# Transposing the 64x64 corner of each attention row tile on VectorE instead of TensorE

## The chip, the cores and the metric

The kernel runs on one core of a Trainium2 chip. The metric is the time of one execution in microseconds (us), measured on the device; smaller is better. Besides the timed runs there is one profiled execution, from which all rows below are taken. The engines are called as in the profile: PE (TensorE, matmuls), PEld (its weight loads), DVE (VectorE), ACT (ScalarE), POOL (GpSimd) and SP (it issues the DMAs).

## The reference, cut to what matters

Three layers follow each other, in float32. The first is a causal attention with 32 heads (batch 4, 8 heads, 576 tokens, 64 columns each):

```
scores = scale * np.matmul(q, k.transpose(0, 1, 3, 2))
scores = np.where(causal, -1000000000.0, scores + np.minimum(bias, 0.0))
attn = np.exp(scores - np.max(scores, axis=-1, keepdims=True))
attn = attn / (np.sum(attn, axis=-1, keepdims=True) + 1e-09)
return np.matmul(attn, v)
```

The second mixes tokens by a rank-32 product and applies a feed-forward layer (512 to 2048 to 512). The third is a causal attention again, with 16 heads (4 batches, 4 experts), whose probabilities are multiplied by a gate; then comes an output product. The change touches only the step between the two products of an attention, where the probabilities have to be transposed so that the sum over keys runs over partitions.

## The kernel before

The program has three stages. The first attention fills the time to about 300 us; beside it, as fillers, run the conversion of weights that arrive as 64-bit words, the token mixing and part of the feed-forward layer. The feed-forward layer alone takes 300 to 680 us. The second attention, with its projections, takes the rest. Both attentions use the class `Attn`.

A head's 576 rows are cut in five row tiles t = 0 to 4. Tile 0 has 64 rows, the others 128; tile t sees 64, 192, 320, 448 or 576 keys (`WID`), because of causality. So tile t has t full blocks of 128x128, and at its right end one 64x64 corner on the diagonal, of which the lower triangle counts. Tile 0 is only a corner.

`run` goes through steps, five for a head. Step i does, in this order: the score product of tile i on PE (`qk`), the transposition of a tile of the head two before it (`tr`, since `LAG` is 10 steps), then on DVE the masked scores with their row maximum (`peak`, L363), on ACT the exponential of the step before (`exp`, L370), and the copies of the transposed tile from PSUM into the buffer `pt` (`evac`, through `cp`: L77 on ACT, L79 on DVE). Once for a head, at its successor's second step, `norm` computes the reciprocals (L375 and L376 on DVE) and has POOL scale all five row tiles (L381). After two heads `push_pv` queues the product with V (L420). The fillers of a step stand behind all that. Each engine works its instructions in program order, so an instruction that waits holds back all behind it.

`TRP` says what the transposing step r = 0 to 4 of a head does: step 0 transposes the full block of tile 1 and the corners of tiles 0 and 1, step 1 tile 2 with its corner, step 2 tile 3 with its corner, step 3 tile 4, step 4 the corner of tile 4. Full blocks are transposed at L393, corners at L396; both go through PE as products with an identity matrix into a PSUM tile `t`, of which there are two in turn. The copy of a corner is a second instruction of `evac`. `ENGA` and `ENGG` name the engine of each copy in the first and the second attention, for even and odd heads; a is ACT, v is DVE. The probabilities lie in two buffers P, for even and odd heads; `pt` has three.

Of the kernel before, what the change touches and what calls it, by code (L numbers as in the profile page):

```python
# [8 lines left out]
F32 = mybir.dt.float32  # L9
# [9 lines left out]
B, H, S, D = 4, 8, 576, 64  # L19
DM, DFF, E, R = 512, 2048, 4, 32  # L20
P = 128
NP = H // 2
NT = 5
# [5 lines left out]
ROWS = [64, 128, 128, 128, 128]  # L29
I0 = [0, 64, 192, 320, 448]  # L30
WID = [64, 192, 320, 448, 576]
OFF = [0, 64, 256, 576, 1024]
PW = 1600
KB = [128, 128, 128, 128, 64]
HALF = S // 2
THIRD = S // 3
# [2 lines left out]
PST = 448  # L39
# [12 lines left out]
STREAM = (((0, 0), (2, -3)), ((-1, 4),), ((0, 1),), ((0, 2), (1, -2)), ((1, -1),), ((0, 3),))  # L52
FAST = (40, 70)

ENGA = ('vaaaaa', 'aavaav')
ULA = "gvgg"
WLE = "g"

HALVES = 152
UFIRST = 161  # L60
WIDE = (7,)
ENGG = ('aaaava', 'aaaava')

GTAB = "kkkkvvvvvqqqq......."
GATE = (9, 5, 2)
OB = "avava"
XG = 0

TRP = ((1, 0, 2), (2, 2, 3), (3, 3, 4), (4, 0, 0), (0, 4, 5))
BG = (1, 1, 0, 2, 1)  # L70
SPLIT = 7
ULF = "vggg"
# [77 lines left out]
def fused_kernel(ctx, tc, qk, v, s, u, vv, w12, wp, out):  # L150
    nc = tc.nc
    cst = ctx.enter_context(tc.tile_pool(name="cst", bufs=1))

    ident = cst.tile([P, P], F32, name="ident")
# [162 lines left out]
    class Attn:  # L317
# [5 lines left out]
        def __init__(self, pools, nq, engines, scale, split=0):  # L323
            self.nq, self.scale, self.split = nq, scale, split
            self.engines = engines
            self.st, self.psq, self.pst = pools
            self.pt = [self.st.tile([P, PTW], F32, name=f"pt{i}") for i in range(3)]
            self.stat, self.P = [], []
# [4 lines left out]
            for i in range(2):  # L333
                self.P.append(self.st.tile([P, PW], F32, name=f"P{i}"))
                nc.gpsimd.memset(self.P[i][0:64, 0:64], 0.0)
            self.pvq = []

        def clear(self, i):


            nc.gpsimd.memset(free_ap(self.pt[i][64:128], 0, [[PST + P, NT], [1, 64]]), 0.0)

        def qk(self, n, t):
            q1, k1, q2, k2 = self.pair_ready(n)
# [11 lines left out]
        def peak(self, n, t, view):  # L356

            M, W = ROWS[t], WID[t]
            stat = self.stat[n % 3]
            po, mk = self.P[n % 2][P - M:, OFF[t]:OFF[t] + W], mask[P - M:, S - W:]  # L360
            if len(view.shape) > 2:
                po, mk = (x.rearrange("p (a b) -> p a b", a=2) for x in (po, mk))
            nc.vector.tensor_tensor_reduce(out=po, in0=view, in1=mk, scale=-self.scale, scalar=3.0e38, op0=OP.add,  # L363
                                           op1=OP.min, accum_out=stat[P - M:, 0, t:t + 1])

        def exp(self, n, t):
            M, W = ROWS[t], WID[t]
            stat = self.stat[n % 3]
            po = self.P[n % 2][P - M:, OFF[t]:OFF[t] + W]
            nc.scalar.activation(out=po, in_=po, func=AF.Exp, scale=-1.0, bias=stat[P - M:, 0, t:t + 1],  # L370
                                 accum_out=stat[P - M:, 1, t:t + 1])

        def norm(self, n):
            stat = self.stat[n % 3]
            nc.vector.tensor_scalar(out=stat[:, 2, :], in0=stat[:, 1, :], scalar1=1e-9, scalar2=None, op0=OP.add)  # L375
            nc.vector.reciprocal(out=stat[:, 2, :], in_=stat[:, 2, :])  # L376
            gate = self.heads[n].get("gate")
            for t in range(NT):
                r0 = P - ROWS[t]
                pv = self.P[n % 2][r0:, OFF[t]:OFF[t] + WID[t]]  # L380
# [3 lines left out]
        def tr(self, n, r):  # L384

            ps = self.pst.tile([P, 512], F32, tag="t", name=f"t_{n}_{r}")
            Pn = self.P[n % 2]
            t, a, e = TRP[r]  # L390
            for kb in range(t):
                c0 = OFF[t] + P * kb
                nc.tensor.transpose(ps[:, P * kb:P * kb + P], Pn[:, c0:c0 + P], ident)  # L393
            for k in range(a, e):
                c0, x = OFF[k] + WID[k] - 64, P * (t + k - a)
                nc.tensor.transpose(ps[0:64, x:x + P], Pn[:, c0:c0 + 64], ident)  # L396
            return ps

        def evac(self, n, r, ps):
            pt = self.pt[n % 3]  # L400
            t, a, e = TRP[r]
            if t:
                cp(nc, self.engines[n % 2][r], free_ap(pt[:, :], I0[t], [[PST, t], [1, P]]), ps[:, :P * t])
# [36 lines left out]
        def run(self, pair_ready, pv_done, heads, fillers):  # L440
            self.pair_ready, self.pv_done, self.heads = pair_ready, pv_done, heads
            n = len(self.heads) * NT
            i = 0
            while i < n + self.LAG or self.pvq:
                j = i - self.LAG
                view = self.qk(i // NT, i % NT) if i < n else None
                ps = self.tr(j // NT, j % NT) if 0 <= j < n else None
                if i < n:
                    self.peak(i // NT, i % NT, view)
                if 1 <= i <= n:  # L450
                    self.exp((i - 1) // NT, (i - 1) % NT)
# [12 lines left out]
                i += 1  # L464
# [465 lines left out]
    with ExitStack() as cx:  # L930
# [148 lines left out]
        def g_out(b, kb):  # L1079
# [10 lines left out]
            if b < B - 1:  # L1090
                ob = d2.tile([P, DM], F32, tag="ob", name=f"ob_{b}_{kb}")
            else:
                ob = attn.P[kb % 2][:, DM * (kb // 2):DM * (kb // 2) + DM]
# [126 lines left out]
```

## Time and profile before

| | us |
|---|---|
| median of 3 timed runs (851.15 to 851.56) | 851.36 |
| the profiled execution's own time | 849.59 |
| its span, first to last instruction | 847.8 |
| PE busy | 804.4 |
| PEld busy | 743.4 |
| DVE busy | 522.2 |
| ACT busy | 478.3 |
| POOL busy | 329.7 |

Busy time is time in which the engine executes at least one instruction. A matmul and the load of its weights overlap, and so do neighbouring matmuls, so PE's busy time is not its load in columns. An idle engine costs time only where the others wait for it.

### The profile page before, as it was taken

The numbers are of one execution on the slowest core, as the hardware profiler recorded it, in microseconds if no ns is written. First come the engines' busy times: TensorE is split into PE (matmuls) and PEld (weight loads), VectorE is DVE, ScalarE is ACT, GpSimd is POOL, SyncE is SP. The second block draws the span as 40 slices with busy tenths as digits, with TensorE's granted clock in tenths as the row PEclk, the third lists the DMA queues.
The fourth block names the chain that finished last, engine by engine and source line by source line (L and its number), as shares of the span: only waits on it lengthen the run. The fifth ranks groups of instructions, "written<-read, shape, count | busy, mean of one in ns | idle before, by whom it ended". The sixth has DMA issues, their size and how long they took to land.

```text
span 847.8 us, 17359 instructions
## 1 busy us (share of the span) xinstructions
PE 804.4 (95%) x6068; PEld 743.4 (88%) x6068; DVE 522.2 (62%) x1547; ACT 478.3 (56%) x1446; POOL 329.7 (39%) x498
## 2 busy tenths in 40 slices
PE   4898799999999999999999999999999989999997
PEld 3676588988888799999999999999999989898875
DVE  7778876786665457646554664464456775656541
ACT  6788777776676445334434443443333576666672
POOL 6656655453453335223422442232333043322241
PEclk9999999999999999999999999999999999999999
DMA  7877566646651151112121221110000221212121
GB/s 212 220 214 208 167 171 187 198 134 169 184 134 44 37 210 51 50 27 55 45 63 26 77 59 42 50 39 26 1 1 2 43 44 29 67 42 54 53 65 62
DMA packets 35897, 75.48 MB, mean 89 GB/s; under 512 B 4584, under 2 KB 8168, under 8 KB 35780
## 3 DMA queue, kind: packets, MB, share of 16 engines
q1 hardware_dynamic: 35812, 74.39, 32.2%
q8 instruction: 48, 0.79, 0.4%
q14 instruction: 37, 0.30, 0.1%
HBM read 38.93 MB, written 8.55 MB: 56 GB/s over the span
## 4 chain that ended last, share of the span: by engine, by line
PE 77%; DVE 5%; ACT 3%; POOL 2%; issue 2%; DMA 0%; SPq 0%; POOLq 0%; DVEq 0%; ACTq 0%
PE hps L836 21%; PE facc L854 21%; PE pv L420 6%; PE qkp L1064 5%; PE t L393 4%; PE facc L298 3%; PE ops L1087 3%; PE hps L284 3%; PE vps L997 3%; PE qk L353 2%; PE qk L352 2%; PE t L396 2%; POOL P L381 2%; DVE P L363 1%; ACT pt L77 1%
## 5 line engine op out<-in xcount | busy, mean ns | idle before, releaser
L268 POOL TENSOR_TENSOR ul<-uT,uh 128x288 fp32r<-128x288 f32 x126 | 101.7, 826 | 172.0 <-ACT uh L267 149.0
L370 ACT ACTIVATE P<-P,stat 64x64 f32<-64x64 f32 (+4 forms) x240 | 133.7, 557 | 44.1 <-DVE stat L363 42.0
L841 DVE SCALAR_TENSOR_TENSOR hl<-hps,hh 128x288 fp32r<-128x288 f32 x110 | 50.4, 458 | 150.0 <-ACT hh L840 150.0
L381 POOL TENSOR_SCALAR P<-P,stat 64x64 f32<-64x64 f32 (+4 forms) x160 | 101.4, 648 | 104.6 <-DVE stat L376 58.1
L363 DVE CUSTOM_DVE_ANT_0 P<-qk,mask 64x64 f32<-64x64 f32 (+4 forms) x240 | 116.4, 487 | 37.6 <-PE qk L353 21.9
L840 ACT ACTIVATE hh<-hps 128x288 fp32r<-128x288 f32 x110 | 45.0, 409 | 147.9 <-PE hps L836 147.6
L77 ACT ACTIVATE pt<-t 64x64 f32<-64x64 f32 (+5 forms) x304 | 89.8, 336 | 41.3 <-PE t L396 35.3
L836 PE MATMUL hps<-uh,wl 128*128 128x288 f32 x376 | 111.2, 296 | 0.0
L836 PE MATMUL hps<-ul,wh 128*128 128x288 f32 x376 | 111.1, 296 | 0.0
L854 PE MATMUL facc<-hh,wh 128*128 128x288 f32 x376 | 111.1, 296 | 0.0
L836 PE MATMUL hps<-uh,wh 128*128 128x288 f32 x376 | 111.0, 295 | 0.0
L854 PE MATMUL facc<-hh,wl 128*128 128x288 f32 x376 | 110.9, 295 | 0.0
L854 PE MATMUL facc<-hl,wh 128*128 128x288 f32 x376 | 110.8, 295 | 0.0
L352 PE MATMUL qk<-R,L 128*128 128x288 f32 (+4 forms) x288 | 94.9, 334 | 16.4 <-DVE L L577 9.6
L393 PE MATMUL t<-ident,P 128*128 128x128 f32 x480 | 88.1, 282 | 11.4 <-ACT pt L77 4.8
L381 POOL TENSOR_SCALAR P<-P,stat,pt 64x64 f32<-64x64 f32 (+4 forms) x80 | 48.5, 620 | 113.1 <-DVE stat L376 57.6
L393 PEld LDWEIGHTS t<-ident,P 128*128 128x128 f32 x480 | 58.8, 142 | 23.3 <-issue 9.4
L352 PEld LDWEIGHTS qk<-R,L 128*128 128x128 f32 x288 | 57.0, 198 | 23.9 <-issue 11.8
L420 PE MATMUL pv<-pt,V 128*64 128x288 f32 (+4 forms) x752 | 76.9, 344 | 0.0
L191 POOL TENSOR_TENSOR wl<-c_a_w,wh 128x256 fp32r<-128x256 f32 x56 | 43.7, 781 | 76.8 <-ACT wh L188 74.2
L836 PEld LDWEIGHTS hps<-uh,wl 128*128 128x128 f32 x376 | 70.9, 189 | 0.0
L854 PEld LDWEIGHTS facc<-hh,wl 128*128 128x128 f32 x376 | 70.9, 188 | 0.0
(186 smaller groups left out, 2145.6 us busy)
## 6 DMA issues: line engine op xcount, KB each, us to landing
c_raw_w<-in_w_dram SPq DMA_DIRECT2D x64, 256.0 KB
uT<-in_qk_dram SPq DMA_DIRECT2D x15, 576.0 KB
L<-HI SPq DMA_DIRECT2D x28, 288.0 KB
V<-in_v_dram SPq DMA_DIRECT2D x16, 320.0 KB
R<-HI SPq DMA_DIRECT2D x14, 288.0 KB
R<-uT SPq DMA_DIRECT2D x14, 288.0 KB
L<-uT SPq DMA_DIRECT2D x14, 288.0 KB
aD<-stage SPq DMA_DIRECT2D x6, 576.0 KB
```

The lines of the kernel that those rows point to most:

```text
L77: nc.scalar.activation(out=out, in_=in_, func=AF.Copy)
L268: eng.tensor_tensor(out=l_, in0=src, in1=h_.bitcast(F32), op=OP.subtract)
L352: nc.tensor.matmul(ps[:, bk, :w], lhsT=q1[:, rows], rhs=k1[:, c0:c0 + w], start=True, stop=False)
L363: nc.vector.tensor_tensor_reduce(out=po, in0=view, in1=mk, scale=-self.scale, scalar=3.0e38, op0=OP.add, op1=OP.min, accum_out=stat[P - M: ...
L370: nc.scalar.activation(out=po, in_=po, func=AF.Exp, scale=-1.0, bias=stat[P - M:, 0, t:t + 1], accum_out=stat[P - M:, 1, t:t + 1])
L381: nc.gpsimd.tensor_scalar(out=pv, in0=pv, scalar1=stat[r0:, 2, t:t + 1], scalar2=1.0 if gate is None else gate(t)[r0:], op0=OP.mult, op1=O ...
L393: nc.tensor.transpose(ps[:, P * kb:P * kb + P], Pn[:, c0:c0 + P], ident)
L420: nc.tensor.matmul(out[64 * hh:64 * hh + 64, lo - a:e - a], lhsT=V(hh, kb), rhs=pt[:, PST * kb + lo:PST * kb + e], start=kb == 0, stop=kb ...
L836: nc.tensor.matmul(ps, lhsT=w[:, 0, cs], rhs=x, start=i == 0, stop=i == 11)
L840: nc.scalar.activation(out=hh, in_=ps, func=AF.Relu)
L841: nc.vector.scalar_tensor_tensor(out=hl, in0=ps, scalar=0.0, in1=hh.bitcast(F32), op0=OP.max, op1=OP.subtract)
L854: nc.tensor.matmul(accs[c][d], lhsT=w[:, 1, cs], rhs=x, start=f == fs[0] and i == 0, stop=f == fs[-1] and i == 2)
```

## The change

The corners are no longer transposed by PE. `corners` has DVE transpose them in blocks of 32x32 directly from P to `pt`, both in SBUF: the two blocks on the diagonal of a corner and the one under it; the fourth is all zeros, and `clear` zeroes its place once. One instruction takes the same block of three tiles (0 to 2, at step 0) or two tiles (3 and 4, at step 2), so there are three instructions at either step. For that the two buffers P become one, in which the corners of a head lie at equal distances. PE transposes tiles 1, 2, 4 and 3 at steps 0 to 3 and nothing at step 4. All copies out of the PSUM tiles `t` are made by ACT.

```
-ENGA = ('vaaaaa', 'aavaav')
+ENGA = ('aaaa', 'aaaa')
-ENGG = ('aaaava', 'aaaava')
+ENGG = ('aaaa', 'aaaa')
-TRP = ((1, 0, 2), (2, 2, 3), (3, 3, 4), (4, 0, 0), (0, 4, 5))
+TRP = (1, 2, 4, 3)
+CORNERS = {0: (0, 3), 2: (3, 5)}
...
             nc.gpsimd.memset(free_ap(self.pt[i][64:128], 0, [[PST + P, NT], [1, 64]]), 0.0)
+            nc.gpsimd.memset(free_ap(self.pt[i][32:64], 0, [[PST + P, NT], [1, 32]]), 0.0)
...
-            for k in range(a, e):
-                c0, x = OFF[k] + WID[k] - 64, P * (t + k - a)
-                nc.tensor.transpose(ps[0:64, x:x + P], Pn[:, c0:c0 + 64], ident)
...
-            if e > a:
-                cp(nc, self.engines[n % 2][r], free_ap(pt[0:64], (PST + P) * a, [[PST + P, e - a], [1, 64]]),
-                   free_ap(ps[0:64], P * t + 64, [[P, e - a], [1, 64]]))
+        def corners(self, n, a, e):
+
+            c0, step = DIAG[n % 2]
+            pt = self.pt[n % 3]
+            for q, k in ((0, 0), (32, 0), (32, 32)):
+                nc.vector.transpose(out=free_ap(pt[k:k + 32], (PST + P) * a + q, [[PST + P, e - a], [1, 32]]),
+                                    in_=free_ap(self.P[64 + q:96 + q], c0 + step * a + k, [[step, e - a], [1, 32]]))
...
-                ps = self.tr(j // NT, j % NT) if 0 <= j < n else None
+                ps = self.tr(j // NT, TRP[j % NT]) if 0 <= j < n and j % NT < len(TRP) else None
+                if 0 <= j < n and j % NT in CORNERS:
+                    self.corners(j // NT, *CORNERS[j % NT])
```

On PE, in the middle of the first attention, steps 0, 2, 3 and 4 of one head; `qk` are score tiles, `t` the PSUM tiles of the transpositions. Before:

```order
L393 MATMUL t_0_2063<-ident,P_114 128x128
L396 MATMUL t_0_2063<-ident,P_114 64x128 x2
...
L393 MATMUL t_2_2132<-ident,P_114 128x128 x3
L396 MATMUL t_2_2132<-ident,P_114 64x128
L352 MATMUL qk_3_2145<-R_1_127,L_1_125 128x448
L353 MATMUL qk_3_2145<-HI,L_1_128 128x448
L393 MATMUL t_3_2148<-ident,P_114 128x128 x4
...
L396 MATMUL t_4_2183<-ident,P_114 64x128
```

And on PE at the same places of the change:

```order
L394 MATMUL t_1_1999<-ident,P 128x128
...
L394 MATMUL t_4_2066<-ident,P 128x128 x4
L357 MATMUL qk_3_2081<-R_1_124,L_1_122 128x448
L358 MATMUL qk_3_2081<-HI,L_1_125 128x448
L394 MATMUL t_3_2084<-ident,P 128x128 x3
```

The five corner transpositions of the head are gone, and tile 4 is transposed before tile 3 (`t` is numbered by the step before, and by the row tile now).

On DVE, from the same head's step 0 to its step 2, before (`ISA` is `peak`, in two instructions; the rows of other lines are fillers and the reciprocals):

```order
L363 ISA P_114,stat_108<-qk_0_2060,mask 64x64
L363 ISA stat_108 64x1
L79 COPY pt_106<-t_0_2063 128x128
L79 COPY pt_106<-t_0_2063 64x2x64
L113 SCALAR_TENSOR_TENSOR pt_107<-pt_105,pt_106 128x256
L253 TENSOR_TENSOR uT<-mo_1_1_2078,uT 128x288
...
L494 TENSOR_TENSOR uT<-uT,HI 128x576
L649 TENSOR_TENSOR stage_2058<-facc_1_2118,uT 128x288
L363 ISA P_114,stat_108<-qk_2_2129,mask 128x320
L363 ISA stat_108 128x1
```

And the same stretch of DVE in the change:

```order
L406 STREAM_TRANSPOSE pt_106<-P 32x3x32 x3
L368 ISA P,stat_108<-qk_0_1996,mask 64x64
L368 ISA stat_108 64x1
L115 SCALAR_TENSOR_TENSOR pt_107<-pt_105,pt_106 128x256
L255 TENSOR_TENSOR uT<-mo_1_1_2014,uT 128x288
...
L497 TENSOR_TENSOR uT<-uT,HI 128x576
L652 TENSOR_TENSOR stage_1994<-facc_1_2052,uT 128x288
L406 STREAM_TRANSPOSE pt_106<-P 32x2x32 x3
L368 ISA P,stat_108<-qk_2_2063,mask 128x320
L368 ISA stat_108 128x1
```

The copies behind `peak` are gone, and the transposes of the corners stand right ahead of the `peak` of tiles 0 and 2.

## Rows read from the trace of the kernel before

**Rows 1.** The page's first part: busy us, share of the span, instructions.
```profile
PE 804.4 (95%) x6068; PEld 743.4 (88%) x6068; DVE 522.2 (62%) x1547; ACT 478.3 (56%) x1446; POOL 329.7 (39%) x498
```

**Rows 2.** Busy time by stretch: length; PE, PEld, DVE, ACT, POOL; clock, DMA share, GB/s.
```profile
20.00:120.00 100.00, 84.80 (x606) 65.66 (x607) 78.37 (x260) 79.70 (x271) 61.56 (x90) 0.98 0.72 195
120.00:280.00 160.00, 157.00 (x1261) 141.29 (x1261) 112.50 (x365) 114.00 (x368) 77.00 (x120) 1.00 0.56 149
280.00:300.00 20.00, 17.84 (x149) 14.05 (x148) 6.95 (x20) 9.73 (x29) 6.92 (x11) 1.00 0.31 104
680.00:848.00 168.00, 158.46 (x1184) 138.51 (x1182) 89.67 (x321) 104.27 (x321) 50.69 (x89) 1.00 0.19 51
```

**Rows 3.** The same of tile t alone: transpositions (PE, PEld), copies (DVE, ACT).
```profile
20.00:120.00 100.00, 33.23 (x186) 20.61 (x186) 7.43 (x26) 21.66 (x74) 0.98 0.72 195
120.00:280.00 160.00, 44.69 (x267) 29.52 (x267) 9.92 (x34) 31.69 (x108) 1.00 0.56 149
280.00:300.00 20.00, 4.36 (x27) 2.87 (x27) 1.15 (x4) 3.48 (x12) 1.00 0.31 104
680.00:848.00 168.00, 39.55 (x240) 25.90 (x240) 3.40 (x16) 32.94 (x112) 1.00 0.19 51
```

**Rows 4.** The chain of waits that ended last, by line, from 120 to 280 us.
```profile
by line: PE facc L298 16.6%; PE hps L284 14.9%; PE pv L420 11.1%; PE t L393 9.2%; PE qk L353 7.2%; PE qk L352 6.8%; PE t L396 5.4%; POOL P L381 5.3%; PE mx L227 3.6%; issue 3.1%; PE mt L239 2.9%; PE mo L250 1.7%; ACT pt L77 1.6%; POOL ul L2
```

**Rows 5.** The same chain from 680 to 848 us.
```profile
by line: PE qkp L1064 19.5%; PE pv L420 15.3%; PE ops L1087 15.2%; PE t L393 9.6%; PE vps L997 8.5%; PE qk L353 5.1%; PE qk L352 4.8%; PE t L396 4.4%; issue 2.6%; ACT pt L77 2.0%; DVE P L363 2.0%; ACT P L370 1.7%; POOL P L381 1.7%; DVE L L1
```

**Rows 6.** Pieces of the chain in order of time: start, us, engine and line.
```profile
152.20 0.11 PE qk L353
152.31 0.17 PE t L393
152.48 0.22 PE t L396 x2
152.69 0.27 PE mo L250 x2
```

**Rows 7.** Groups by shape, DVE: busy us, mean ns of one, idle before, releaser.
```profile
L79 DVE COPY pt<-t 128x384 f32<-128x384 f32 x16 | 8.8, 552 | 0.8 <-PE t L396 0.7
L79 DVE COPY pt<-t 64x64 f32<-64x64 f32 x32 | 6.7, 209 | 3.6 <-PE t L396 3.5
L79 DVE COPY pt<-t 128x128 f32<-128x128 f32 x16 | 4.7, 292 | 0.5
L79 DVE COPY pt<-t 64x128 f32<-64x128 f32 x16 | 4.4, 273 | 0.0
L375 DVE TENSOR_SCALAR stat<-stat 128x5 f32<-128x5 f32 x48 | 9.2, 191 | 6.6 <-ACT P L370 6.4
L668 DVE TENSOR_TENSOR U<-c_a_u,U 128x160 fp32r<-128x160 f32 x2 | 0.8, 438 | 0.0
```

**Rows 8.** Groups by shape, ACT's copies out of t.
```profile
L77 ACT ACTIVATE pt<-t 64x64 f32<-64x64 f32 x112 | 23.1, 206 | 1.2 <-PE t L396 1.1
L77 ACT ACTIVATE pt<-t 128x384 f32<-128x384 f32 x32 | 15.6, 486 | 28.4 <-PE t L396 28.4
L77 ACT ACTIVATE pt<-t 128x128 f32<-128x128 f32 x32 | 8.5, 266 | 1.9 <-PE t L396 1.5
L77 ACT ACTIVATE pt<-t 64x128 f32<-64x128 f32 x32 | 8.3, 260 | 0.0
```

**Rows 9.** POOL in order of time: start, us of the five scalings of a head.
```profile
22.54 4.01 POOL L381 TENSOR_SCALAR P<-P,stat 64x64 f32<-64x64 f32 x5 [0.46 <-DVE stat L376]
...
190.76 3.32 POOL L381 TENSOR_SCALAR P<-P,stat 64x64 f32<-64x64 f32 x5 [1.26 <-DVE stat L376]
```

**Rows 10.** DVE in order of time: start, us.
```profile
21.16 0.48 DVE L79 COPY pt<-t 128x128 f32<-128x128 f32 x2
...
28.06 0.49 DVE L363 CUSTOM_DVE_ANT_0 P<-qk,mask 128x320 f32<-128x320 f32 x1
...
201.03 0.23 DVE L363 CUSTOM_DVE_ANT_0 P<-qk,mask 64x64 f32<-64x64 f32 x1
```

More of the change, by code (lines that the diff above doesn't have):

```diff
@@ L31 @@
 WID = [64, 192, 320, 448, 576]
-OFF = [0, 64, 256, 576, 1024]
-PW = 1600
+SLOT = 640
+OFF = [[SLOT * t for t in range(5)], [SLOT * (5 - t) - WID[t] for t in range(5)]]
+DIAG = [(WID[0] - 64, SLOT + P), (SLOT * 5 - 64, -SLOT)]
 KB = [128, 128, 128, 128, 64]
@@ L327, in __init__ @@
             self.pt = [self.st.tile([P, PTW], F32, name=f"pt{i}") for i in range(3)]
-            self.stat, self.P = [], []
+            self.stat = []
             for i in range(3):
@@ L332, in __init__, with rows @@
                 self.stat.append(t)
-            for i in range(2):
-                self.P.append(self.st.tile([P, PW], F32, name=f"P{i}"))
-                nc.gpsimd.memset(self.P[i][0:64, 0:64], 0.0)
+            self.P = self.st.tile([P, SLOT * NT], F32, name="P")
             self.pvq = []
+        def rows(self, n, t):
+            c0 = OFF[n % 2][t]
+            return self.P[P - ROWS[t]:, c0:c0 + WID[t]]
         def clear(self, i):
             nc.gpsimd.memset(free_ap(self.pt[i][64:128], 0, [[PST + P, NT], [1, 64]]), 0.0)
+            nc.gpsimd.memset(free_ap(self.pt[i][32:64], 0, [[PST + P, NT], [1, 32]]), 0.0)
         def qk(self, n, t):
@@ L359, in peak @@
             stat = self.stat[n % 3]
-            po, mk = self.P[n % 2][P - M:, OFF[t]:OFF[t] + W], mask[P - M:, S - W:]
+            po, mk = self.rows(n, t), mask[P - M:, S - W:]
             if len(view.shape) > 2:
@@ L366, in exp @@
         def exp(self, n, t):
-            M, W = ROWS[t], WID[t]
+            M = ROWS[t]
             stat = self.stat[n % 3]
-            po = self.P[n % 2][P - M:, OFF[t]:OFF[t] + W]
+            po = self.rows(n, t)
             nc.scalar.activation(out=po, in_=po, func=AF.Exp, scale=-1.0, bias=stat[P - M:, 0, t:t + 1],
@@ L379, in norm, with tr @@
                 r0 = P - ROWS[t]
-                pv = self.P[n % 2][r0:, OFF[t]:OFF[t] + WID[t]]
+                pv = self.rows(n, t)
                 nc.gpsimd.tensor_scalar(out=pv, in0=pv, scalar1=stat[r0:, 2, t:t + 1],
                                         scalar2=1.0 if gate is None else gate(t)[r0:], op0=OP.mult, op1=OP.mult)
[L384 to L390, printed above, removed]
+        def tr(self, n, t):
+            ps = self.pst.tile([P, 512], F32, tag="t", name=f"t_{n}_{t}")
+            Pt = self.rows(n, t)
             for kb in range(t):
-                c0 = OFF[t] + P * kb
-                nc.tensor.transpose(ps[:, P * kb:P * kb + P], Pn[:, c0:c0 + P], ident)
-            for k in range(a, e):
-                c0, x = OFF[k] + WID[k] - 64, P * (t + k - a)
-                nc.tensor.transpose(ps[0:64, x:x + P], Pn[:, c0:c0 + 64], ident)
+                nc.tensor.transpose(ps[:, P * kb:P * kb + P], Pt[:, P * kb:P * kb + P], ident)
             return ps
         def evac(self, n, r, ps):
+            t = TRP[r]
+            cp(nc, self.engines[n % 2][r], free_ap(self.pt[n % 3][:, :], I0[t], [[PST, t], [1, P]]), ps[:, :P * t])
+        def corners(self, n, a, e):
+            c0, step = DIAG[n % 2]
             pt = self.pt[n % 3]
-            t, a, e = TRP[r]
-            if t:
-                cp(nc, self.engines[n % 2][r], free_ap(pt[:, :], I0[t], [[PST, t], [1, P]]), ps[:, :P * t])
-            if e > a:
-                cp(nc, self.engines[n % 2][r], free_ap(pt[0:64], (PST + P) * a, [[PST + P, e - a], [1, 64]]),
-                   free_ap(ps[0:64], P * t + 64, [[P, e - a], [1, 64]]))
+            for q, k in ((0, 0), (32, 0), (32, 32)):
+                nc.vector.transpose(out=free_ap(pt[k:k + 32], (PST + P) * a + q, [[PST + P, e - a], [1, 32]]),
+                                    in_=free_ap(self.P[64 + q:96 + q], c0 + step * a + k, [[step, e - a], [1, 32]]))
         def push_pv(self, n, half=None):
@@ L1092, in g_out @@
             else:
-                ob = attn.P[kb % 2][:, DM * (kb // 2):DM * (kb // 2) + DM]
+                ob = attn.P[:, DM * kb:DM * kb + DM]
             cp(nc, OB[kb], ob[:m], ps[:m])
```

## The prediction

> **What bounds the kernel now.** I read the page's busy times first, then the busy time by stretch, then the chain of waits. PE is busy 95% of the span, the next engine 62% [rows 1], but this is a mean over stages. From 20 to 120 us of the first attention PE is busy 85 of 100 us, DVE 78, ACT 80, and the DMAs 0.72: nothing is full, and they wait for each other in turn. From 120 to 280 us PE is busy 157 of 160 us while DVE has 112.5 and ACT 114. In the second attention, 680 to 848 us, PE has 158.5 of 168 us and DVE 89.7 [rows 2]. So in the two later stretches PE sets the pace, in the first one not clearly. The chain says the same: from 120 to 280 us nearly all its larger entries are PE lines, and the corner transpositions (L396) hold 5.4% of it [rows 4]; from 680 us on they hold 4.4% [rows 5]. 300 to 680 us has no transposition of an attention and isn't touched.
>
> **What is removed on PE.** A corner transposition lies in the pipeline, so its own duration says little; on the chain two of them take 0.22 us, 0.11 us each [rows 6]. Five for each of 48 heads are 240, so at most 240 x 0.11 = 26.4 us, 0.55 us a head. A head has 15 transpositions before, so the counts [rows 3] give the heads in each stretch: 186/15 = 12.4 heads from 20 to 120 us, 17.8 from 120 to 280, 1.8 from 280 to 300, and 16 in the second attention. In PE time these are 6.8, 9.8, 1.0 and 8.8 us. What of it is on the path is read from the chain: 5.4% of 160 us = 8.6 us and 4.4% of 168 us = 7.4 us [rows 4, 5]. From 280 to 300 us I count all of the 1.0. From 20 to 120 us, where PE idles 15%, I take nothing, with the bounds below.
>
> **What is moved and added on DVE.** It loses its copies out of PSUM: 16 of 128x384, 16 of 128x128, 16 of 64x128 and 32 of 64x64, 8.8 + 4.7 + 4.4 + 6.7 = 24.6 us [rows 7]. By the engine table 21.2 us of that are in the first attention (0.66 us a head; half of the 64x64 ones are there) and 3.4 in the second (0.21 a head). It gains six transposes a head, three with 96 and three with 64 elements in a partition. The trace has no such instruction. Below, it can't cost less than the smallest DVE operation from SBUF to SBUF, 0.191 us for 5 elements; above, I take 0.438 us, a DVE operation from SBUF to SBUF with 160 elements. I choose the plain copies of the same width, the rows nearest in kind (they move data without arithmetic) and size: 0.209 us for 64, and for 96 the middle between 64 and 128, 0.241 us [rows 7]. That is 3 x 0.241 + 3 x 0.209 = 1.35 us a head, 64.8 us in all. Net, DVE has 0.69 us more a head in the first attention and 1.14 us more in the second. From 120 to 280 us it goes from 112.5 to 112.5 + 17.8 x 0.69 = 125 us, below PE's 157 - 9.8 = 147; in the second attention from 90 to 108 us, below PE's 150. From 20 to 120 us it goes to 78.4 + 8.6 = 87 us and PE to 78: there DVE becomes the busiest.
>
> On the timeline two copies that follow each other end in 0.48 us, while their means sum to 0.565 [rows 7, 10]: neighbours overlap by about 0.08 us. The Trainium skill, page "VectorE: DVE Perf Modes", section "Two Vector instructions with no wait between them", says that an instruction that begins in another quarter of the partitions than its predecessor read or wrote waits until all earlier ones have ended; these transposes change quarters each time, so the rule would let none overlap. By the rule the 64.8 us stand in full; without it, 288 x 0.08 = 23 us of them would go, and the DVE rival below would be less likely. The same page of the Trainium skill, section "The three transpose paths", gives 311 ns for VectorE on a 128x128 bf16 tile, dearer than the copy of that width. An estimate from it, less 0.001 us per element, is 0.28 and 0.25 us, some 11 us more over all heads; no row here shows it.
>
> **ACT.** It loses 112 copies of 64x64 and 32 of 64x128 (23.1 + 8.3 us) and takes over 16 of 128x384 and 16 of 128x128 (7.8 + 4.3 us) [rows 8]: 19 us less. ACT is not what the chain passes through (1.6% and 2.0%, rows of the copies, [rows 4, 5]), so I count nothing for it. A PSUM tile t is now always freed by ACT; there are four of them to a head instead of five, which offsets that.
>
> **Waits that the order makes.** The transposes read P after POOL's scaling, and on DVE `peak` and all fillers of the step queue behind them; PE's next score products need the PSUM tiles that `peak` frees. So the question is whether POOL is done. The tightest place I found is at the start: the scaling of a head begins at 22.54 us and ends at 26.55, and the `peak` ahead of which the second group of transposes stands begins at 28.06: 1.5 us to spare. Later the five end at 194.08 and the `peak` of the right step begins at 201.03, 7 us later [rows 9, 10]. I count no wait; if the cover were gone, a late scaling would hold DVE for what it is late. The second change of order is that tile 3 is transposed at step 3, right ahead of the `peak` that overwrites tile 3 of that buffer: this `peak` waits for three more transpositions, 0.33 us at 0.11 each. In return the `peak` of tile 0 no longer waits for three transpositions (0.17 + 0.22 us, [rows 6]) and that of tile 4 not for its corner. I count the two as equal. The extra zeroing on POOL is six instructions at the two starts, hidden behind the loads and projections there.
>
> **What is given back.** Where the chain leaves PE it goes through DVE's reciprocals to POOL's scaling and on. POOL's L381 has 5.3% of 160 us = 8.5 us and 1.7% of 168 us = 2.9 us [rows 4, 5], at 3.32 us a head [rows 9] 2.6 and 0.9 heads. If each such passage meets DVE's net addition of its head, it costs 2.6 x 0.69 + 0.9 x 1.14 = 2.8 us.
>
> **Sum.** 8.6 + 7.4 + 1.0 - 2.8 = 14.2 us less. The profiled execution's own time of 849.59 us becomes 835.4; the median of the runs shown lies 1.77 us above that execution, so on its scale 851.36 - 14.2 = 837.2 us.
>
> **The rivals.**
> *First, PE's whole saving arrives,* also from 20 to 120 us, and the overlap on DVE hides its addition: 26.4 us, 825.0. For it speaks that DVE loses waits for PE, and that ACT loses 19 us. Against it speaks that PE idles 15% in the first stretch [rows 2], so there its saving turns into more idle time, as far as others hold it. Chance 0.1.
> *Second, DVE's addition is on the path in the early stretch.* There it is the busiest after the change. If 12.4 x 0.69 = 8.6 us come on top and the rest stands, 5.6 us are left, 845.8; if in addition the `peak` of tile 3 comes 0.33 us late in each of the 17.8 heads from 120 to 280 us (5.9 us), it is 851.7, no change. For it speaks that ACT and DVE are as full there as PE; against it, that DVE still idles 22 of 100 us. Chance 0.17.
> *Third, slower: a transpose of 32x32 blocks is dear.* At the upper bound of 0.438 us, DVE has from 20 to 120 us 78.4 + 12.4 x (2.63 - 0.66) = 103 us, more than the stretch itself, and from 120 to 280 us 112.5 + 17.8 x 1.97 = 147.6, as much as PE. If an engine that sets the pace reaches 93% in the attention (PE's 242 of 260 us from 20 to 280), the two stretches take 110.5 and 158.7 us, +10.5 and -1.3; with 5 us still won in the second attention the sum is +4 us, 855.5. It decides from about 0.42 us on: there the two stretches take 109 and 156.5 us, +9.1 and -3.5, and the 5 us are used up. Against it speaks that the copy of 64x128 takes 0.273 us [rows 7], far below. Chance 0.12.
>
> **Chances and range.** My forecast, 829 to 844 us, has 0.61. The three rivals have 0.10, 0.17 and 0.12. A measurement of this kernel can tell 0.2%, 1.7 us, from no change. Faster by more than that: 0.61 + 0.10 + 0.10 of the second = 0.81; within it: 0.07 of the second = 0.07; slower: 0.12. The range reaches from 828, somewhat short of the first rival, to 851, which takes in most of the second; it leaves out the third and half of the first.
>
> **What the profile of the changed kernel would show.** PE has 240 fewer instructions and no transposition of 64 columns. DVE has 288 transposes; their mean, near 0.225 us or not, decides between the forecast and the third rival. DVE's busy time is 522.2 + 64.8 - 24.6 = 562 us, ACT's 459. If I am right, PE is still near 98% busy in the middle of the first attention and in the second, and both stretches are shorter by about 0.5 us a head. In the second rival's case PE's idle time before 120 us grows and DVE's shrinks. POOL as the releaser of a transpose would show that the scaling is late after all. The prediction would be wrong, too, if the score products waited for PSUM tiles that a later `peak` frees: then PE's idle time before L357 would grow.

## The result and the profile after

The changed kernel takes 856.51 us (median of 10 runs, 853.68 to 861.55), the kernel before beside it 851.56 (10 runs, 850.0 to 854.48): ratio 1.0053, interval 1.003 to 1.0077. It is slower by about half a per cent, 4.5 us, where 14 us less were forecast. The profiled execution took 853.68 us, with a span of 851.6; it is one of the two fastest of the ten. Below, a ratio is turned into microseconds by 851 us.

The first part of its page answers to [rows 1] (busy us, share of the span, instructions):

```profile
PE 788.3 (93%) x5828; PEld 724.1 (85%) x5828; DVE 573.4 (67%) x1755; ACT 467.3 (55%) x1334; POOL 327.9 (39%) x500
```

PE has lost 240 instructions and 16 us of busy time, and DVE has gained 51 us; no engine is near full on average. The busy time by stretch answers to [rows 2] (length; PE, PEld, DVE, ACT, POOL; granted clock, DMA share, GB/s):

```profile
20.00:120.00 100.00, 80.90 (x529) 61.51 (x529) 88.04 (x298) 77.10 (x239) 60.17 (x90) 0.93 0.71 195
120.00:280.00 160.00, 149.13 (x1156) 129.89 (x1155) 128.06 (x434) 110.64 (x327) 73.76 (x117) 1.00 0.56 149
280.00:300.00 20.00, 17.52 (x149) 14.49 (x148) 11.52 (x36) 10.54 (x29) 7.94 (x13) 1.00 0.12 33
680.00:848.00 168.00, 155.27 (x1133) 135.25 (x1131) 114.49 (x414) 97.86 (x279) 49.88 (x89) 0.98 0.20 52
```

In the middle of the first attention, where PE was busy 157 of 160 us, it now idles 10.9 us. DVE, at 128 us, idles 32. The granted clock is 1.00 in both rows, so it isn't the clock. PE was relieved and didn't use the relief: before, it did 1261 - 5 x 17.8 = 1172 instructions there other than corners, now 1156. It waits. The chain of waits says for whom, from 120 to 280 us (the row that answers to [rows 4]) and from 680 to 848 us (to [rows 5]); "issue" is time in which an engine waits for nothing that the profile shows:

```profile
by line: PE facc L300 13.1%; PE pv L421 11.2%; PE hps L286 10.5%; DVE pt L406 7.2%; DVE P L368 6.7%; issue 5.7%; PE t L394 5.1%; PE qk L357 4.2%; PE qk L358 3.9%; DVE xl L233 3.2%; ACT pt L79 2.7%; ACT P L375 2.5%; DVE uT L497 2.2%; POOL P 
...
by line: PE qkp L1067 16.2%; issue 15.1%; POOL P L386 11.4%; PE ops L1090 9.3%; PE pv L421 9.2%; PE t L394 4.6%; PE vps L1000 4.4%; ACT P L375 4.4%; DVE pt L406 4.3%; PE qk L358 3.4%; DVE P L368 3.0%; PE qk L357 3.0%; DVE yl L1130 1.4%; DVE
```

The 5.4% of the corner transpositions on PE has been replaced by 7.2% of the transposes on DVE (L406), and DVE's `peak` (L368) has come beside it with 6.7%. In the second attention POOL's scaling (L386), which had 1.7% in the row of before, has 11.4%. Of the 15.1% "issue" there, 25.4 us, two pieces of 9.29 us (at 714.88) and 7.07 us (at 802.45) are idle time of POOL ahead of a scaling. Both times POOL starts 0.17 us after the reciprocal that it needs has ended, so it waited for DVE, which the view doesn't name, and PE was busy 16.1 of these 16.4 us: this part of the chain doesn't say what PE lacked. For the whole run the chain's shares by engine (page, part 4) are:

```profile
PE 65%; DVE 16%; issue 6%; ACT 5%; POOL 5%; DMA 2%; SPq 1%; POOLq 0%; DVEq 0%; ACTq 0%
```

Of before it was PE 77% and DVE 5%. The new instructions by shape (busy us, mean ns of one, idle before, releaser; they answer to the copies of [rows 7]):

```profile
L406 DVE STREAM_TRANSPOSE pt<-P 32x96 f32<-32x96 f32 x144 | 38.8, 269 | 20.1 <-POOL P L386 17.8
L406 DVE STREAM_TRANSPOSE pt<-P 32x64 f32<-32x64 f32 x144 | 33.9, 236 | 7.8 <-POOL P L386 5.3
```

They cost 72.7 us, against 64.8 in the prediction, and in front of them DVE waits 23.1 us for POOL, where no wait was counted.

### The profile page after: what moved, and what is told of

It is laid out like the page before. It is cut to its first block, busy times and chain, and to the rows that moved or that the text cites. A ratio compares the mean times of both kernels' runs of the same rounds, so it can differ in the third digit from the quotient of the medians.

```text
span 851.6 us, 16772 instructions
## 1 busy us (share of the span) xinstructions
PE 788.3 (93%) x5828; PEld 724.1 (85%) x5828; DVE 573.4 (67%) x1755; ACT 467.3 (55%) x1334; POOL 327.9 (39%) x500
## 4 chain that ended last, share of the span: by engine, by line
PE 65%; DVE 16%; issue 6%; ACT 5%; POOL 5%; DMA 2%; SPq 1%; POOLq 0%; DVEq 0%; ACTq 0%
PE hps L839 21%; PE facc L857 20%; PE pv L421 5%; PE qkp L1067 4%; DVE P L368 3%; POOL P L386 3%; DVE pt L406 3%; PE facc L300 3%; PE t L394 2%; PE hps L286 2%; ACT P L375 2%; PE ops L1090 2%; PE vps L1000 2%; PE qk L357 2%; PE qk L358 2%
## 5 line engine op out<-in xcount | busy, mean ns | idle before, releaser
L386 POOL TENSOR_SCALAR P<-P,stat 64x64 f32<-64x64 f32 (+4 forms) x160 | 99.5, 636 | 116.2 <-DVE stat L381 63.3
L368 DVE CUSTOM_DVE_ANT_0 P<-qk,mask 64x64 f32<-64x64 f32 (+4 forms) x240 | 115.4, 487 | 15.6 <-PE qk L358 3.8
L394 PE MATMUL t<-ident,P 128*128 128x128 f32 x480 | 90.6, 290 | 15.6 <-ACT pt L79 12.4
L79 ACT ACTIVATE pt<-t 128x128 f32<-128x128 f32 x192 | 81.2, 427 | 23.7 <-PE t L394 22.9
L386 POOL TENSOR_SCALAR P<-P,stat,pt 64x64 f32<-64x64 f32 (+4 forms) x80 | 47.8, 609 | 115.5 <-DVE stat L381 50.9
L406 DVE STREAM_TRANSPOSE pt<-P 32x64 f32<-32x64 f32 (+1 forms) x288 | 72.7, 252 | 27.9 <-POOL P L386 23.1
L394 PEld LDWEIGHTS t<-ident,P 128*128 128x128 f32 x480 | 60.7, 146 | 25.7 <-issue 8.0
L421 PEld LDWEIGHTS pv<-pt,V 128*64 128x64 f32 x752 | 48.7, 139 | 28.4 <-issue 4.1
```

What stands on the lines that cost most here:

```text
L394: nc.tensor.transpose(ps[:, P * kb:P * kb + P], Pt[:, P * kb:P * kb + P], ident)
L406: nc.vector.transpose(out=free_ap(pt[k:k + 32], (PST + P) * a + q, [[PST + P, e - a], [1, 32]]), in_=free_ap(self.P[64 + q:96 + q], c0 + s ...
L421: nc.tensor.matmul(out[64 * hh:64 * hh + 64, lo - a:e - a], lhsT=V(hh, kb), rhs=pt[:, PST * kb + lo:PST * kb + e], start=kb == 0, stop=kb ...
```

## How the lateness travels

This is a reading of one trace; the experiments below test parts of it. Near the beginning, DVE, ACT and PE in order of time (start, us, idle time before in brackets, with its releaser); first DVE:

```profile
26.71 0.61 DVE L368 CUSTOM_DVE_ANT_0 P<-qk,mask 128x448 f32<-128x448 f32 x1
...
27.42 0.74 DVE L368 CUSTOM_DVE_ANT_0 P<-qk,mask 128x576 f32<-128x576 f32 x1
...
28.46 0.83 DVE L406 STREAM_TRANSPOSE pt<-P 32x96 f32<-32x96 f32 x3
29.43 0.23 DVE L368 CUSTOM_DVE_ANT_0 P<-qk,mask 64x64 f32<-64x64 f32 x1
```

then ACT:

```profile
27.36 0.67 ACT L375 ACTIVATE P<-P,stat 128x448 f32<-128x448 f32 x1 [1.52 <-DVE stat L368]
...
28.30 0.76 ACT L375 ACTIVATE P<-P,stat 128x576 f32<-128x576 f32 x1
...
29.05 0.26 ACT L79 ACTIVATE pt<-t 128x128 f32<-128x128 f32 x1
```

and PE:

```profile
26.86 0.30 PE L358 MATMUL qk<-HI,L 68*128 68x320 f32 x1
29.45 1.01 PE L394 MATMUL t<-ident,P 128*128 128x128 f32 x4 [2.29 <-ACT pt L79]
```

DVE hardly idles in this stretch (3.25 of 3.4 us busy from 26.0 to 29.4 us). ACT's exponential waits 1.52 us for `peak`; the copy out of tile t stands behind two exponentials in ACT's order; PE's next transpositions wait 2.29 us for that copy to free their PSUM tile. So an engine that has idle time on average holds up another, which holds up PE. Summed from 0 to 300 us, in the view of the waits (waiting line, line waited for: us, times, longest):

```profile
ACT P L375 <- DVE stat L368: 36.9, 58, 2.7
...
PEld qk L357 <- DVE stat L368: 12.0, 16, 2.9
...
PE t L394 <- ACT pt L79: 9.9, 11, 2.3
...
PE qk L357 <- DVE stat L368: 5.4, 11, 1.4
```

The same lines before:

```profile
ACT P L370 <- DVE stat L363: 17.5, 32, 2.3
...
PE t L393 <- ACT pt L77: 3.3, 5, 1.4
...
PEld qk L352 <- DVE stat L363: 2.6, 3, 1.7
...
PE qk L352 <- DVE stat L363: 0.4, 1, 0.4
```

and in `none`, the change without the transposes (next section):

```profile
ACT P L375 <- DVE stat L368: 15.1, 21, 3.0
...
PE t L394 <- ACT pt L79: 4.5, 7, 1.5
...
PEld qk L357 <- DVE stat L368: 1.3, 2, 0.8
...
PE qk L357 <- DVE stat L368: 0.6, 1, 0.6
```

So the waits for `peak` grow with DVE's transposes: the score products, which need the PSUM tiles that `peak` frees, wait 17.4 us for it instead of 3.0. In the second attention, 680 to 852 us, the same view has DVE itself among those that wait:

```profile
ACT P L375 <- DVE stat L368: 39.8, 31, 4.2
DVE pt L406 <- POOL P L386: 23.1, 22, 1.9
```

In DVE's order of time there is one such place, and in POOL's beside it:

```profile
723.86 0.18 DVE L381 RECIPROCAL stat<-stat 128x5 f32<-128x5 f32 x1
725.83 0.84 DVE L406 STREAM_TRANSPOSE pt<-P 32x96 f32<-32x96 f32 x3 [1.79 <-POOL P L386]
727.34 0.23 DVE L406 STREAM_TRANSPOSE pt<-P 32x64 f32<-32x64 f32 x1 [0.67 <-POOL P L386]
...
724.21 3.10 POOL L386 TENSOR_SCALAR P<-P,stat,pt 64x64 f32<-64x64 f32 x5 [9.32 <-issue]
```

In 8 of the 16 heads the transposes stand right behind the reciprocals whose scaling they need, so they wait for POOL. The order in which they were issued is not the code's. The manual order of the first attention is closed before the second (`sched.close()`, L931), and from there a scheduler sets the order. On DVE, in the second attention of the change (the reciprocal starts at 766.02 us):

```
L381 RECIPROCAL stat_8734<-stat_8734 128x5
L406 STREAM_TRANSPOSE pt_8729<-P 32x3x32 x3
L1005 COPY pt_8727<-vps_1_10086 128x4
L406 STREAM_TRANSPOSE pt_8729<-P 32x2x32 x2
L368 ISA P,stat_8730<-qk_1_10101,mask 128x192
```

The prediction had looked at this order in the first attention alone, where the transposes come several steps behind the reciprocals.

## The experiments

**Neither engine, and both.** Two theories at first: the transposes' time on DVE holds the loop up (load); or PE idles more, and its granted clock falls to half (clock). `none` takes the corners from both engines, `both` leaves them on both.

```diff
 none:
...
-                if 0 <= j < n and j % NT in CORNERS:
-                    self.corners(j // NT, *CORNERS[j % NT])
 both, in tr:
...
+            for x, k in enumerate({1: (0, 1), 2: (2, 3), 3: (4,)}.get(t, ())):
+                c0 = OFF[n % 2][k] + WID[k] - 64
+                nc.tensor.transpose(ps[0:64, P * (t + x):P * (t + x) + P], self.P[:, c0:c0 + 64], ident)
```

> The change without any corner work: DVE's 288 transposes are left out as well, the corners of pt stay zero, so the diagonal blocks of the probabilities are missing from the sums. Load theory (DVE's 72.7 us of transposes eat the saving of PE): without them the saving shows, 832 to 840 us, 12 to 20 under before. Clock theory (PE idles more, and the granted clock falls to half): PE has even less to do than in the change, the mean clock stays at 0.985 or lower and the time is 846 us or more.

> The change, with the 240 corner transpositions of PE put back for nothing: their results aren't copied out. Load theory: in the first attention DVE sets the pace, so PE's 17 us there cost little, under 4 us; in the second attention up to 8.8 us come on top: 857 to 866 us. Clock theory: PE idles less, the clock goes back to 0.995 or more and the time falls to 852 us or less.

Measured: `none` 834.51 us (ratio 0.9821, 0.9794 to 0.9848), `both` 864.82 (1.0171, 1.0153 to 1.0188), beside 850.54 of before. PE's relief brings 15.2 us together with that of DVE and ACT, which have lost their copies of the corners too (DVE has 20 us less than before). The transposes on DVE then cost the distance from `none` to the change, 1.0053 - 0.9821, 19.7 us (17 to 23 by the intervals). With them on DVE, PE's relief is worth 1.0171 - 1.0053, 10 us (7.5 to 12.5). The page and the windows of `none`:

```profile
PE 781.9 (94%) x5828; PEld 723.3 (87%) x5828; DVE 502.5 (60%) x1467; ACT 467.9 (56%) x1334; POOL 329.9 (40%) x500
...
120.00:280.00 160.00, 154.46 (x1219) 137.70 (x1216) 105.79 (x336) 114.41 (x339) 78.21 (x123) 0.99 0.56 149
```

PE has as many instructions as in the change, ACT the same busy time, and the granted clock of the two profiled executions is as good as equal (0.989 and 0.988; as a mean of all runs 0.987 and 0.982). DVE differs by 70.9 us, no other engine by more than 6.4, and PE is 154 of 160 us busy again. `none` has the one buffer P and the order of the tiles from the change, so these aren't the cause. Nor do the transposes slow others down: a `peak` of 576 columns takes 0.750 us in the change and 0.751 in `none`, POOL's scaling of the first attention 101.8 and 102.1 us in all. Both times lie where the theory of load had them; that of the clock had 846 us or more for `none`, and 852 or less for `both`. So what takes the relief away comes from the transposes on DVE: their time and their waits.

**One attention at a time.** The five corners of an attention stay on PE as before, or go to DVE.

```diff
...
+TRP5 = ((1, 0, 2), (2, 2, 3), (3, 3, 4), (4, 0, 0), (0, 4, 5))
...
+            self.pe = len(engines[0]) > 4
...
-            t, a, e = TRP[r]
+            t, a, e = TRP5[r] if self.pe else (TRP[r], 0, 0)
```

> DVE transposes the corners in the first attention alone; the second does it as before, on PE with the old engines for the copies. Load theory: the loss lies in the first attention, where DVE is busy 88 of 100 us after the change: 853 to 857 us. Theory of POOL (transposes that wait 23.1 us for POOL's scaling, all of them in the second attention, are the cause): 843 to 849 us.

> DVE transposes the corners in the second attention alone; the first is as before. Load theory: PE sets the pace there and DVE has room, so the time is 843 to 850 us, under before. Theory of POOL: the waits of DVE for the scaling are here, and the time is 854 us or more.

Measured: first attention alone 856.6 us (1.0069, 1.0053 to 1.0084), second alone 851.67 (1.0017, 1.0 to 1.0035). The loss is in the first, 5.9 us; the second wins nothing, though PE is relieved there of as much in each head. That falls between the two theories of `second_dve`, neither of which expected it.

**Held back.** The transposes are placed behind the last `peak` in DVE's order, which moves them away from the reciprocals; in the second attention alone (`second_late`), and in the change (`after_late`).

```diff
...
+            self.last = nc.vector.tensor_tensor_reduce(...)
...
-                    self.corners(...)
+                    with tc.issue_after(self.last.ins) if self.split == 0 else ExitStack():
+                        self.corners(...)
```

> DVE transposes the corners in the second attention alone (as second_dve, 851.7 us), and there they are held, in DVE's order, behind the peak of the step before, where the code has them; in second_dve they stand right behind the reciprocals and wait for POOL. Theory that the waits for POOL's scaling ate the saving of the second attention (23.1 us of DVE): most of the 10 us come back, 841 to 847 us. Theory that the load of DVE alone did it: 849 to 853 us.

> The change, with the transposes of the second attention held back in the same way; the first attention as in the change. Theory of the waits: 846 to 852 us, that is, the change's 856.5 less what second_late wins over second_dve. Theory of load: 854 to 858 us.

`second_late` takes 848.38 us (0.997, 0.9955 to 0.9985), 4.0 us less than `second_dve` (2 to 6 by the intervals), again between the two theories. In its view of the waits, 680 to 852 us, what was 22.4 us in `second_dve` is

```profile
DVE pt L420 <- POOL P L391: 2.5, 2, 1.8
```

The wait for POOL was real, and the order made it. `after_late` takes 855.65 us (1.0058, 1.0038 to 1.0078): in the median nothing that can be told from the change, though its view has the wait down from 23.1 to 2.5 us as well. The cut by stages below shows why in part.

**Order and size in the first attention.** `first_behind` puts the first group behind the `peak` of the step before and the second behind the `peak` of tile 2, instead of ahead of that of tiles 0 and 2. `first_one_group` takes all five corners in one group, three transposes of 160 elements a head instead of three of 96 and three of 64; in the kernel that ran, the order of the full transpositions was still that of the change.

```diff
 first_behind, behind evac:
...
+                if self.split and 0 <= j + 1 < n and (j + 1) % NT == 0:
+                    self.corners((j + 1) // NT, 0, 3)
+                if self.split and 0 <= j < n and j % NT == 2:
+                    self.corners(j // NT, 3, 5)
 first_one_group:
+GROUP = {0: (0, 5)}
...
-                if 0 <= j < n and j % NT in CORNERS:
+                if 0 <= j < n and j % NT in (GROUP if self.split else CORNERS):
...
```

> The change, with the transposes of the first attention one peak later or earlier: the first group stands behind the peak of the step before, the second behind the peak of tile 2 instead of ahead of it; the load of DVE is the same. Theory that DVE's load is what costs in the first attention: 855 to 859 us, as the change. Theory that the place ahead of the peak costs (it delays the peak by the group's 0.75 us): 848 to 853 us.

> The change, with the five corners of a head of the first attention in one group of three transposes (160 elements each) at step 0 instead of two groups of three (96 and 64), and tile 3 transposed before tile 4. Extrapolated from the 269 and 236 ns of the change one takes about 335 ns, so DVE has 1.0 us a head instead of 1.5, 16 us less in the first attention. Theory of load: 2 to 6 us under the change, 850 to 854 us. Theory of place: the longer group ahead of one peak costs as much as the two, 855 to 859 us, and if the scaling isn't done by then, more.

`first_behind` takes 854.07 us (1.0038, 1.0024 to 1.0053), `first_one_group` 851.68 (1.0003, 0.9984 to 1.0022). The place won 1.3 us, which can't be told from nothing, and lies between the two theories; fewer and longer transposes give 4.3 us back (2 to 7), by the ratios. In the trace of `first_behind` (of the fastest of its twelve runs, 849.33 us) the score products hardly wait for `peak` any more:

```profile
PEld qk L357 <- DVE stat L368: 2.7, 5, 1.5
...
PE qk L357 <- DVE stat L368: 1.2, 1, 1.2
```

3.9 us instead of 17.4, and yet the time is little less. So that link alone isn't what costs. The page of `first_one_group`, and its transposes by shape:

```profile
PE 792.4 (93%) x5828; PEld 725.6 (85%) x5828; DVE 555.6 (65%) x1659; ACT 466.6 (55%) x1334; POOL 329.8 (39%) x500
...
L407 DVE STREAM_TRANSPOSE pt<-P 32x160 f32<-32x160 f32 x96 | 32.2, 336 | 2.3 <-POOL P L387 0.6
```

DVE has 17.8 us less than in the change: 0.24 us of time for each us of DVE (0.1 to 0.4 by the intervals). The transposes of tiles 3 and 4 also come two steps earlier here, so size isn't tested all by itself.

**ACT's queue, and more on DVE.** `evac_first` puts ACT's copy out of t ahead of the exponential in a step of the first attention, against the link of the chain seen above. `copies_back` gives DVE a part of the copies again (`ENGA = ('vaaa', 'aaav')`): if ACT's copies were what holds PE up, it would be faster, and if DVE's load is, slower.

```diff
 evac_first, ahead of exp:
...
+                if ps is not None and self.split:
+                    self.evac(...)
...
 copies_back:
+ENGA = ('vaaa', 'aaav')
```

> The change, with ACT's copy out of the PSUM tile t ahead of the exponential in each step of the first attention, not behind it. In the change PE's longest idle times before 120 us (2.29, 1.51, 1.96 and 1.49 us) end with such a copy of ACT, and the granted clock is at half right after each. Theory that these late copies matter: the idle times shrink, the mean clock rises from 0.982 to 0.987 or more, 849 to 854 us. Theory of DVE's load alone: 855 to 859 us, since ACT waits for DVE's peak in either order.

> The change, with the copies of full blocks that DVE made before given back to it in the first attention (tile 1 of even heads, tile 3 of odd heads). DVE has 13.5 us more, ACT 12 us less. Theory of DVE's load: 858 to 864 us. Theory that ACT's taking over the copies is what makes PE wait for PSUM tiles: 850 to 855 us.

`evac_first` takes 856.1 us (1.0061, 1.0035 to 1.0086), the same as the change, though in its trace (of the slowest of its ten runs, 864.78 us) PE waits for such copies half as long, 4.7 us for 9.9:

```profile
PE t L394 <- ACT pt L79: 4.7, 5, 1.9
```

That place in ACT's order isn't the cause. (Of PE's long idle times before 120 us in the change, two more, 2.60 and 2.19 us, end with other work than such a copy: a DMA and POOL.) `copies_back` takes 862.42 us (1.0124, 1.0101 to 1.0147), 6.0 us more than the change, though it relieves ACT:

```profile
PE 797.9 (93%) x5828; PEld 728.8 (85%) x5828; DVE 585.9 (68%) x1787; ACT 459.5 (53%) x1302; POOL 326.0 (38%) x500
```

DVE has 12.5 us more, at 0.48 us of time for each (0.3 to 0.7 by the intervals). These are copies out of PSUM, which also wait for PE, so the price isn't one of busy time alone.

**One group everywhere.** All corners of a head in one group and in the order 1, 2, 3, 4, held back in the second attention: the second alone (`second_one_late`), and both (`one_late`).

```diff
...
-CORNERS = {0: (0, 3), 2: (3, 5)}
-TRP = (1, 2, 4, 3)
+CORNERS = {0: (0, 5)}
+TRP = (1, 2, 3, 4)
```

> DVE transposes the corners in the second attention alone, held back as in second_late (848.4 us), in one group of three transposes per head and with tile 3 ahead of tile 4. DVE has 0.5 us less per head, 8 us in all. Theory that what is left of the loss in the second attention is DVE's load: 843 to 847 us. If it is something else (the clock, the wait of PE for POOL's scaling): 847 to 850 us.

> The change with both mends in both attentions: one group of three transposes per head, held back in the second attention. Theory of load and waits, adding what each alone won (4.8 us by the group in the first attention, 1 to 3 us by holding back, 2 to 4 by the group in the second): 844 to 850 us. If the gains overlap, 850 to 853 us.

`second_one_late` takes 846.14 us (0.9942, 0.9921 to 0.9963), 4.9 us less than before, and is the fastest version but for `none`. `one_late` takes 850.55 (0.9986, 0.9968 to 1.0005). That is 5.7 us under the change: with both mends the move costs nothing, and wins nothing either. From 680 to 830 us, `second_one_late`:

```profile
680.00:830.00 150.00, 141.14 (x1045) 123.97 (x1043) 101.17 (x350) 94.72 (x268) 50.63 (x89) 0.98 0.18 48
```

and `second_late`, which differs by the group and the order of the tiles alone:

```profile
680.00:830.00 150.00, 142.23 (x1050) 125.59 (x1050) 109.36 (x404) 94.47 (x268) 48.12 (x87) 0.98 0.20 50
```

With 8.2 us less on DVE, PE gets through no more instructions in the same time. The 2.4 us between the two kernels, by the ratios, come with an uncertainty of 2.2. Nor does a cut by stages show them, though 846.14 us lies where the theory of load had it. The second attention's projections begin with the product `qkp`; in each profiled execution it starts here (us), and the rest takes this long:

| profiled execution | first `qkp` | from there to the end |
|---|---|---|
| before | 651.8 | 196.0 |
| the change | 655.6 | 196.0 |
| `none` | 645.8 | 185.8 |
| `first_dve` | 660.9 | 196.1 |
| `second_dve` | 657.2 | 195.8 |
| `second_late` | 655.2 | 192.7 |
| `after_late` | 659.5 | 194.0 |
| `second_one_late` | 651.9 | 192.9 |

The last column is the second attention, with its projections. There the change is as long as before; what it loses in these executions, 3.8 us, it loses ahead of it. Holding the transposes back is worth 3.1 us there (`second_dve` to `second_late`) and 2.0 (the change to `after_late`); one group adds nothing. The column before it scatters more: `second_dve`, `second_late` and `second_one_late` do the same up to there and lie 5.3 us apart, `after_late` and the change 3.9. The medians of the change and `after_late` are sure to 2.6 us of difference by the intervals, so a gain of 2 us can be hidden there.

**Early heads, late heads.** If the loss were only in the stretch up to 120 us, where DVE is the busiest, the later heads should win what PE is relieved of. The corners go to DVE for the first 12 heads of the first attention alone, or for the 20 others alone; the last kernel adds those 20, in one group, to `second_one_late`.

```diff
...
+            self.pe = (lambda n: pe and not (split and n < 12))
...
```

> DVE transposes the corners of the first 12 heads of the first attention (to about 120 us), PE those of the other 20 and of the second attention. Theory that the loss of the first attention (5.6 us, first_dve) lies where DVE is busiest, before 120 us: 855 to 860 us. Theory that it costs alike in every head: 12/32 of it, 852 to 854 us.

> DVE transposes the corners of heads 12 to 31 of the first attention (from about 120 us), PE those of the first 12 and of the second attention. Theory that the loss lies before 120 us: PE set the pace here, so up to 5 us are won, 845 to 850 us. Theory that it costs alike in every head: 853 to 856 us.

> second_one_late (846.1 us) with the corners of heads 12 to 31 of the first attention on DVE as well, in one group of three transposes per head. Theory that the loss of the first attention lies before 120 us: 838 to 845 us. Theory that it costs alike in every head, and the group of three half of that: 846 to 849 us.

`early_heads` takes 853.99 us (1.0028, 1.001 to 1.0046), `late_heads` 853.34 (1.0014, 0.9993 to 1.0035), `late_heads_second` 848.06 (0.9956, 0.9934 to 0.9978). All three lie where the theory of a cost alike in every head had them. The late heads win nothing; whether they lose isn't settled, their interval reaches just below 1. From 120 to 280 us, where PE was near full, `late_heads` reads like the change, so the idle time of PE there isn't carried over from the first 12 heads, which are those of before:

```profile
120.00:280.00 160.00, 149.90 (x1152) 131.03 (x1151) 127.31 (x431) 109.86 (x326) 73.99 (x116) 0.99 0.56 149
```

## Why the prediction was wrong

*What is given back* is the step that failed: 2.8 us for DVE's net addition (transposes less copies), where the transposes alone cost 19.7, the distance from `none` to the change. The step before it had compared sums of busy time, 125 us on DVE with 147 on PE from 120 to 280 us, and took the engine with less for hidden, but for the few places where the chain went through POOL's scaling. The sums were about right, 128 and 149 us; what was inferred from them wasn't. `peak` on DVE, the exponential on ACT and the transpositions and score products on PE wait for each other within a step, through a few PSUM tiles. DVE doesn't need to be full for its 1.5 us a head to arrive late at the next engine. The prediction's last sign of being wrong came: the score products waited 17.4 us for `peak`, 3.0 before. Measured, a us of transposes costs 0.27 us (19.7 of 72.7, `none` to the change, waits for POOL included; 0.23 to 0.31 by the intervals). The 0.24 of `first_one_group` and the 0.48 of `copies_back` don't differ from that clearly.

*What PE is relieved of* looks right, but isn't shown: 17.0 us were read from the chain, and `none` measured 15.2 (12.9 to 17.5), with DVE's and ACT's copies gone as well. DVE has 20 us less there than before, which would be worth some 5 us at 0.27, an estimate; `both` puts PE's relief at 10 us with the transposes on DVE. In the cut by stages `none` wins 6.0 us up to the first `qkp` and 10.2 behind it, where the chain had 9.6 and 7.4, and 10.2 is more than the 8.8 us of PE time that were there to be saved. So that the sums agree is partly luck.

*Waits that the order makes* failed too, at a place the prediction didn't look at: in the second attention a scheduler set the transposes right behind the reciprocals, and DVE waited 23.1 us for POOL. POOL as releaser was named as what would show it. Taking the wait away was worth 4.0 us with the first attention as before (3.1 in the cut by stages). In the first attention POOL was in time, as forecast. That tile 3 is transposed right ahead of the `peak` that overwrites it did no harm, as forecast: before the 48 peaks of 448 columns DVE waits 0.6 us for it in all.

*The price of a transpose* was somewhat low: 0.269 and 0.236 us for 0.241 and 0.209, 7.9 us more in all, and the third rival's 0.42 us was far off. So this rival had the sign of the result but not its cause. The estimate from the Trainium skill, page "VectorE: DVE Perf Modes", section "The three transpose paths" (0.28 and 0.25), was nearer than the copies of the same width. Its section "Two Vector instructions with no wait between them" agrees with the trace: three transposes of 96 elements in a row take 0.84 us and three of 64 take 0.73, their means sum to 0.81 and 0.71, so none overlaps, as neighbouring copies did.

*The second rival,* DVE's addition on the path, had the mechanism but confined it to the stretch up to 120 us. There its sign came: PE idles 19.1 of 100 us instead of 15.2, DVE 12.0 instead of 21.6. But `late_heads` shows that the later heads don't win their share either. Its 845.8 to 851.7 us were short by that.

*DVE's and ACT's busy time* came out at 573.4 and 467.3 us for 562 and 459. That nothing is counted for ACT stands: it was relieved by 11 us, and `evac_first` and `copies_back` show that its copies aren't what PE lacks.

*Open.* The granted clock, as a mean of all runs, was 0.982 in the change, 0.987 in `none`, and 0.993 to 0.995 in before (the runs beside the other kernels). Over the change's own 10 runs the time rises by about 0.6 us for each 0.001 of clock lost, over those of before by 0.3 to 0.4. By these slopes, an estimate, the clock could hold up to 3 of the 19.7 us between `none` and the change, and 4 to 7 us, as much as the whole loss, between before and the change. No run here separates cause from effect, since idle time of PE comes at each fall (below). It isn't the cause in the stretch from 120 to 280 us, where it was 1.00. Open, too, is which of the links between DVE and PE weighs most: `first_behind` and `evac_first` each relieved one of them, and the time hardly fell.

## What to carry to other kernels

Busy shares don't say whether work that is moved to an engine is hidden: here, between engines that hand tiles to each other in every step, a us cost about a quarter of a us on one that was busy 68 to 88% of the two attentions. Run the kernel once with the work on neither engine: that bounds what the move can win, and its distance to the real change is what the new place costs. Look at the issue order in every region that has a scheduler of its own, and if work must go to such an engine, send it in few, long instructions (4.3 us in the first attention; none seen in the second), and where the receiving engine has the most room: here the second attention, DVE busy 53% before, where `second_one_late` won 4.9 us (3.1 in the cut by stages). That the other engine is full doesn't suffice: from 120 to 280 us PE was busy 98% and DVE 70%, and nothing was won.

## What the runs showed of the hardware

A transpose of 32x32 blocks on DVE has a large fixed part: 236 ns for 64 elements in a partition, 269 for 96, 336 for 160, so about 1.04 ns for an element and 170 ns besides. One of 160 does the work of 505 ns in two.

The granted clock of TensorE fell to half (1.2 of 2.4 GHz) around or right behind an idle time of PE of 1.5 to 2.7 us, for 3.3 to 6.8 us: four times in the change (the fourth at 695.2 us), once before (3.4 us at 107.5 us, behind 2.41 us of idle time). Not every such idle time has one: 2.19 us ahead of 109.41, 2.11 ahead of 251.78 and 1.90 ahead of 818.98 were followed by a clock of 1.00. Three stretches of the change at half clock, and the time ahead of the first, columns as in the windows above:

```profile
26.00:29.40 3.40, 1.16 (x10) 0.90 (x8) 3.25 (x11) 2.04 (x7) 0.61 (x1) 1.00 0.97 244
29.60:32.90 3.30, 3.30 (x15) 2.29 (x16) 3.14 (x15) 3.15 (x11) 2.25 (x5) 0.50 0.99 236
...
43.30:46.60 3.30, 3.25 (x13) 2.44 (x15) 3.09 (x15) 2.94 (x10) 1.74 (x4) 0.50 0.94 227
...
74.00:80.70 6.70, 6.02 (x28) 4.59 (x28) 5.38 (x20) 5.56 (x19) 4.47 (x8) 0.50 0.73 239
```

At 29.4 us PE has just waited 2.29 us for ACT's copy (above), and at half clock it looks full: 3.30 of 3.30 us. So a stretch of idle time can cost more than its own length, and busy time at half clock is no sign of a bound.
